# Taking the weight checks out of the first step of every chunk

## The chip, the cores and the metric

The kernel runs on one core of one Trainium2 chip. The metric is the device time of one execution in microseconds (us). Five engines work side by side, each through its own queue of instructions: TensorE for matrix products (PE in the profile, with its weight loads as PEld), VectorE (DVE), ScalarE (ACT), GpSimd (POOL), and SyncE (SP), which here issues nearly all transfers.

## The reference

An attention layer with a short window and a few always-visible first keys, followed by a two-layer network with softplus. Cut to what matters:

```python
# q, k, v: (B=4, H=8, S=768, D=64); n_sink = 4, window = 128
scores = (q @ k.transpose(0, 1, 3, 2)) / 8
keep = (key < n_sink) | ((0 <= query - key) & (query - key < window))
a = softmax(where(keep, scores, -1e9))            # over the keys
x = (a @ v).transpose(0, 2, 1, 3).reshape(3072, 512)
h = x @ w_in                                      # w_in: 512 x 2048, float64
g = maximum(h, 0) + log1p(exp(-abs(h)))
out = (g @ w_out).astype(float32)                 # w_out: 2048 x 512, float64
```

## The kernel before

The 3072 tokens are cut into 12 chunks of 256. A chunk has 8 **steps**. In step i the kernel works on two chunks at once: head i % 8 of the attention of chunk i // 8, and slice i % 8 (256 of the 2048 hidden columns) of the two dense layers of the chunk before. The loop over i is one long software pipeline; from step 17 on it runs the letters of `Ctx.STEADY` in their order. Each letter is a function and an offset. For this study these matter:

- `U` (`up`, line 474): 24 products of one slice of the first layer into the PSUM tile `h`. `F` (`softplus`, lines 481 to 483): three ScalarE passes into `mt`. `P` (`gate`, line 489, and line 50 or 48 for the cast `gh`), `R` (`residue`, `gl`, line 56): VectorE's part, of the step itself and of the step before. `D` and `E` (`down`, lines 511 to 513): 12 products of the slice of two steps before into `acc`.
- `p` (`split`): `qkh`, `kl` on line 56. `S` (`scores`): line 245 and 246. `T` (`softmax`): lines 258, 264 (VectorE) and 265 (ScalarE). `N` (`normalise`): `sm`, `rc` on VectorE (271, 272), the product with `a` on GpSimd (279).
- `W` (`weights_t`): PE turns the head's attention weights round (line 312, tile `t`), ScalarE makes the high part `th`, VectorE the low part `tl` (line 56), and GpSimd cuts both to the band with four selects (lines 323 and 326) into the tile `pt`. `V` (`values`): PE multiplies, first the sinks (line 342), then the band, which reads `pt` (line 348), both into `x`. `O` (`out`): ScalarE and VectorE (`xt` line 366, `xf` line 367) take `x` away.

Seven of eight steps run the letters in the order `kWRqpUKFSTDPNVOE`. The first step of a chunk (i % 8 = 0) runs `kqWRpSDKTUFNPVEO`: there `U` and `F` come late, behind `S`, `D` and `T`.

Behind the letters of some steps comes a **weight check** (`_weight_check`, line 455). The weights are float64 and are put together from words; one check takes the smallest and the largest magnitude of one half block of weights, two VectorE reductions of 128 x 512 into one column each of `room`. There are 32 half blocks in the list `checks`. Nobody but the flag reads `room`: `_fast_signs` in step 98 folds it with `stats` into a column, `_fast_flag` in step 100 turns that round on PE (line 697) and makes a number of it, which at the very end decides whether a slow general program has to run instead. It does not with these inputs.

PE's and SP's instructions stand in the order in which the code is written; the scheduler may arrange the rest.

Of the kernel before, what the change touches and what calls it, by code (L numbers as in the profile page):

```python
# [20 lines left out]
B, H, S, D = 4, 8, 768, 64  # L21
# [423 lines left out]
def _weight_check(c, s, k, half):  # L445

    if not c.w64:  # L450
        return
    w = c.w[s, k, half][:, 0].rearrange("p n w -> p (n w)")
    o = 2 * (2 * s + k) + half
    for e, op in enumerate((ALU.min, ALU.max)):
        c.nc.vector.tensor_reduce(c.room[:, e, o : o + 1], w, mybir.AxisListType.X, op, apply_absolute_value=True)
# [69 lines left out]
def _fast(c):  # L525
# [8 lines left out]
    lag = 2  # L534
# [11 lines left out]
    checks, dmas = list(halves), list(halves)  # L546
# [57 lines left out]
    def next_sinks(i):  # L604

        k, e = divmod(i + H, H)
        if k <= c.EXACT or k > n:
            return
        if k < n and att[k].first and 0 < e < 6:
            a = att[k]  # L610
            if e < 4:
                (a.load_sinks, a.sinks_high, a.sinks_low)[e - 1]()
            else:
                a.sinks_place(0, e - 4)
        elif att[k - 1].first and k - 1 > c.EXACT and e < 2:
            att[k - 1].sinks_place(1, e)

    def fill(n):

        for _ in range(n):  # L620
            c.nc.tensor.matmul(c.word_ps[0][:, :CT].bitcast(F32), c.sk[:, :P], c.sk[:], start=True, stop=True)
# [27 lines left out]
    with c.tc.manual_schedule():  # L649
        c.word_ps = [c.ps_acc.tile([P, WH], I32, tag=f"acc{e}", name=f"word_ps{e}") for e in range(2)]  # L650
        fill(16)
        for h in (0, 2):
            att[0].load(h)
        _constants(c)
        att[0].load_v(0)
        att[0].load_sinks()
        att[0].load(4)
        att[0].load_v(1)
        att[0].load(6)
        c.turn = 0  # L660
        c.upper = [c.lp.tile([P, WH], I32, tag=f"vs{e}", name=f"upper{e}", bufs=1) for e in range(2)]
        for t in c.upper:
            c.nc.gpsimd.memset(t[:], 0)
        for part in c.START.split():
            parts[part[0]][0](int(part[1:] or 0))
        for i in range(2 * H + 1, (n + 1) * H + lag + 1):
            for part in "JjGL" + c.STEADY[i % H == 0]:
                run, ahead = parts[part]
                run(i + ahead)
            next_sinks(i)  # L670
            if i >= 2 * H + lag and i % 2 == 0 and checks:
                _weight_check(c, *checks.pop(0))
            if i == n * H + lag:
                for e in checks:
                    _weight_check(c, *e)
                _fast_signs(c)
            if i == n * H + 2 * lag:
                _fast_flag(c)


def _fast_signs(c):

    nc = c.nc
    c.col = col = c.const.tile([P, 3], F32, name="flag_col")
    nc.vector.tensor_reduce(col[:, 0:1], c.stats[:, : c.nchunks * CH * H], mybir.AxisListType.X, ALU.max)
    for e, (op, lim, beyond) in enumerate(((ALU.min, 2.0**-119, ALU.is_lt), (ALU.max, 2.0**121, ALU.is_ge))):
        m = col[:, e + 1 : e + 2]
        nc.vector.tensor_reduce(m, c.room[:, e], mybir.AxisListType.X, op)
        nc.vector.tensor_scalar(m, m, lim, BIG, beyond, ALU.mult)
        nc.vector.tensor_tensor(col[:, 0:1], col[:, 0:1], m, ALU.max)  # L690


def _fast_flag(c):

    nc, cp = c.nc, c.const
    row = c.ps_t.tile([1, P], F32, tag="t", name="flag_row")
    nc.tensor.transpose(row[:], c.col[:, 0:1], c.ident[:])
    f = cp.tile([1, 2], F32, name="flag_f")
    ok, u = f[:, 0:1], f[:, 1:2]
    nc.vector.tensor_reduce(ok, row[:], mybir.AxisListType.X, ALU.max)  # L700
    nc.vector.tensor_scalar(ok, ok, 9.0e8, None, ALU.is_lt)
    for src, lim, op in ((c.ns, float(NS), ALU.is_le), (c.wd, 1.0, ALU.is_ge), (c.wd, float(P), ALU.is_le)):
        nc.vector.tensor_scalar(u, src[:1], lim, None, op)
        nc.vector.tensor_tensor(ok, ok, u, ALU.mult)
    c.flag = cp.tile([1, 1], I32, name="flag_i")
    nc.vector.tensor_copy(c.flag[:], ok)
# [126 lines left out]
def _kernel(tc, a, out):  # L833
# [7 lines left out]
    with ExitStack() as keep:  # L841
        c.const = keep.enter_context(tc.tile_pool(name="const", bufs=1))
        c.wp = keep.enter_context(tc.tile_pool(name="wp", bufs=1))
        c.w, c.raw, c.top, c.word = {}, {}, {}, {}
        c.ident = c.const.tile([P, P], F32, name="ident")
        c.stats = c.const.tile([P, B * H * NB], F32, name="stats")
        c.room = c.const.tile([P, 2, 4 * FP], F32, name="room")
        nc.gpsimd.memset(c.room[:], 1.0)
        c.sk = c.const.tile([P, CT], F32R, name="sk")
        ones = c.room[:].rearrange("p a b -> p (a b)").unsqueeze(1).broadcast_to([P, CT // 64, 64])  # L850
        _zero(nc, c.sk[:].rearrange("p (a b) -> p a b", b=64), ones)
        with ExitStack() as st:
            pool = lambda n, bufs: st.enter_context(tc.tile_pool(name=n, bufs=bufs))
            psum = lambda n, bufs: st.enter_context(tc.tile_pool(name=n, bufs=bufs, space=bass.MemoryType.PSUM))
            c.xp, c.mp, c.stg = pool("xp", 2), pool("mp", 2), pool("stg", 4)
            c.lp, c.ap, c.sp = pool("lp", 2), pool("ap", 2), pool("sp", 2)
            c.ps_acc, c.ps_h = psum("ps_acc", 1), psum("ps_h", 2)
            c.ps_s, c.ps_t, c.ps_x = psum("ps_s", 2), psum("ps_t", 1), psum("ps_x", 1)
            with tc.manual_schedule(engines=ORDERED):
                _fast(c)  # L860
        ok = nc.values_load(c.flag[:1, :1], min_val=0, max_val=1)
        with tc.If(ok < 1):
            _general(c)
# [77 lines left out]
```

## Time and profile before

| | |
|---|---|
| time, median of 3 runs | 724.29 us (724.26 to 725.24) |
| the profiled execution's own time | 724.42 us |
| its span, first to last instruction | 722.7 us |
| granted TensorE clock | 0.998 |
| PE / PEld / DVE / ACT / POOL busy | 97% / 86% / 80% / 63% / 52% |
| checks | 64 reductions, steps 18, 20, ... 80 |

The span is read with step numbers in mind: step 24 begins near 162 us, step 40 near 274 us, step 88 near 612 us, and a step lasts about 7 us. The last letters of `U` are those of step 103, near 705 us. Idle time that a row shows in square brackets is that of the engine just before the instruction, with what ended it.

### The profile page before, as it was taken

The numbers are of one execution on the slowest core, as the hardware profiler recorded it, in microseconds if no ns is written. First come the engines' busy times: TensorE is split into PE (matmuls) and PEld (weight loads), VectorE is DVE, ScalarE is ACT, GpSimd is POOL, SyncE is SP. The second block draws the span as 40 slices with busy tenths as digits, with TensorE's granted clock in tenths as the row PEclk, the third lists the DMA queues.
The fourth block names the chain that finished last, engine by engine and source line by source line (L and its number), as shares of the span: only waits on it lengthen the run. The fifth ranks groups of instructions, "written<-read, shape, count | busy, mean of one in ns | idle before, by whom it ended". The sixth has DMA issues, their size and how long they took to land.

```text
span 722.7 us, 13866 instructions
## 1 busy us (share of the span) xinstructions
PE 701.4 (97%) x4535; PEld 624.5 (86%) x4535; DVE 581.5 (80%) x1693; ACT 452.5 (63%) x1104; POOL 373.8 (52%) x676
## 2 busy tenths in 40 slices
PE   7889999999999999999999999999999999999996
PEld 5577789988998898998999899898888898999995
DVE  6899988888987987888888987988888887855332
ACT  4679847666666666766666666666665766643431
POOL 5867485655455564655544564564555465452000
PEclk9999999999999999999999999999999999999999
DMA  9887713221221411321321322222221312100000
GB/s 309 289 303 223 197 49 90 58 72 58 81 66 37 122 49 50 109 64 46 101 68 49 98 59 67 80 75 64 75 74 52 96 51 77 60 12 1 30 2 34
DMA packets 40875, 63.21 MB, mean 87 GB/s; under 512 B 4634, under 2 KB 22362, under 8 KB 40794
## 3 DMA queue, kind: packets, MB, share of 16 engines
q1 hardware_dynamic: 40506, 61.97, 28.0%
q8 instruction: 38, 0.62, 0.4%
q14 instruction: 43, 0.35, 0.2%
q10 hardware_dynamic: 288, 0.26, 0.1%
HBM read 55.93 MB, written 6.29 MB: 86 GB/s over the span
## 4 chain that ended last, share of the span: by engine, by line
PE 69%; DVE 14%; ACT 8%; issue 4%; POOL 3%; DMA 2%; SPq 0%; ACTq 0%; POOLq 0%; DVEq 0%
PE h L474 28%; PE acc L513 9%; PE acc L511 9%; PE acc L512 9%; PE x L348 5%; PE t L312 2%; PE s L245 2%; PE s L246 2%; DVE gl L56 2%; POOL pt L323 2%; ACT a L265 1%; PE x L342 1%; DVE kl L56 1%; ACT mt L482 1%; DVE mt L489 1%
## 5 line engine op out<-in xcount | busy, mean ns | idle before, releaser
L474 PE MATMUL h<-xh,wi 128*128 128x256 f32 x1536 | 253.8, 288 | 0.0
L474 PEld LDWEIGHTS h<-xh,wi 128*128 128x128 f32 x1536 | 211.2, 191 | 1.6 <-issue 0.5
L279 POOL TENSOR_SCALAR a<-a,rc 128x128 f32<-128x128 f32 x178 | 69.3, 402 | 188.9 <-DVE rc L272 150.5
L474 PE MATMUL h<-xl,wi 128*128 128x256 f32 x768 | 154.6, 283 | 0.0
L511 PE MATMUL acc<-wo,gh 128*128 128x512 f32 x384 | 151.8, 395 | 0.0
L513 PE MATMUL acc<-wo,gl 128*128 128x512 f32 x384 | 151.0, 393 | 0.7 <-DVE gl L56 0.7
L512 PE MATMUL acc<-wo,gh 128*128 128x512 f32 x384 | 150.7, 393 | 0.0
L474 PEld LDWEIGHTS h<-xl,wi 128*128 128x128 f32 x768 | 119.7, 192 | 0.0
L489 DVE SCALAR_TENSOR_TENSOR mt<-h,mt 128x512 f32<-128x512 f32 x96 | 66.0, 687 | 63.3 <-ACT mt L483 54.5
L481 ACT ACTIVATE mt<-h 128x512 f32<-128x512 f32 x96 | 57.1, 595 | 93.8 <-PE h L474 93.8
L265 ACT ACTIVATE a<-a,stats 128x136 f32<-128x136 f32 x192 | 76.4, 399 | 58.2 <-DVE stats L264 57.7
L513 PEld LDWEIGHTS acc<-wo,gl 128*128 128x128 f32 x384 | 72.2, 188 | 17.5 <-DVE gl L56 1.1
L511 PEld LDWEIGHTS acc<-wo,gh 128*128 128x128 f32 x384 | 72.3, 188 | 12.8 <-issue 0.3
L56 DVE TENSOR_TENSOR gl<-mt,gh 128x512 fp32r<-128x512 f32 x96 | 79.9, 832 | 0.3
L512 PEld LDWEIGHTS acc<-wo,gh 128*128 128x128 f32 x384 | 72.3, 188 | 8.9
L323 POOL TENSOR_SCALAR_AFFINE_SELECT pt<-tl 128x256 fp32r<-128x256 f32 x80 | 60.1, 751 | 29.6 <-DVE tl L56 28.9
L323 POOL TENSOR_SCALAR_AFFINE_SELECT pt<-th 128x256 fp32r<-128x256 f32 (+1 forms) x96 | 44.2, 460 | 36.1 <-ACT th L48 33.1
L482 ACT ACTIVATE mt<-mt 128x512 f32<-128x512 f32 x96 | 60.7, 633 | 3.1
L483 ACT ACTIVATE mt<-mt 128x512 f32<-128x512 f32 x96 | 60.7, 632 | 3.0
L48 ACT CAST qkh<-qk 128x656 fp32r<-128x656 f32 x80 | 59.5, 744 | 2.5 <-DMA qk<-qk 2.5
L56 DVE TENSOR_TENSOR kl<-qk,qkh 128x400 fp32r<-128x400 f32 x80 | 52.7, 658 | 2.5
L56 DVE TENSOR_TENSOR tl<-t,th 128x256 f32<-128x256 f32 x80 | 33.2, 415 | 24.5 <-ACT th L48 24.1
(185 smaller groups left out, 1245.2 us busy)
## 6 DMA issues: line engine op xcount, KB each, us to landing
qk<-qk SPq DMA_DIRECT2D x160, 164.0 KB, 3.0
vr<-v SPq DMA_DIRECT2D x32, 192.0 KB, 2.7
out<-o SPq DMA_DIRECT2D x24, 256.0 KB, 2.3
vr<-v SPq DMA_DIRECT2D x16, 128.0 KB, 2.4
q<-q SPq DMA_DIRECT2D x7, 256.0 KB, 4.6
k<-k SPq DMA_DIRECT2D x8, 200.0 KB, 4.6
wi00r<-w SPq DMA_DIRECT2D x1, 511.8 KB, 5.3
wi01r<-w SPq DMA_DIRECT2D x1, 511.8 KB
```

Of the source, the lines that this page charges most:

```text
L48: nc.scalar.copy(out, in_)
L56: (nc.vector if eng == "V" else nc.gpsimd).tensor_tensor(out, a, b, ALU.subtract)
L265: nc.scalar.activation(a, a, AF.Exp, bias=nm, scale=-1.0, accum_out=sm[:, j : j + 1])
L279: (nc.vector if eng == "V" else nc.gpsimd).tensor_scalar(a, a, rc[:, j : j + 1], 0.0, ALU.mult, ALU.add)
L323: nc.gpsimd.affine_select(pt[:, e, :, 1], src[:], [[0, CH], [1, P]], ALU.is_ge, 0.0, base=0, channel_multiplier=-1)
L474: nc.tensor.matmul(h[:, j], wt, x, start=k == 0, stop=k >= len(prods) - 2, skip_group_check=True)
L482: nc.scalar.activation(t[:], t[:], AF.Exp, scale=-1.0)
L483: nc.scalar.activation(t[:], t[:], AF.Ln, bias=1.0)
L489: nc.vector.scalar_tensor_tensor(t[:], h[:], 0.0, t[:], ALU.max, ALU.add)
L511: nc.tensor.matmul(acc[:], gh[:, j, q], wh, start=f == 0, stop=False, skip_group_check=True)
L512: nc.tensor.matmul(acc[:], gh[:, j, q], wl, start=False, stop=False, skip_group_check=True)
L513: nc.tensor.matmul(acc[:], gl[:, j, q], wh, start=False, stop=f == 2 * FP - 1, skip_group_check=True)
```

## The change

The test that starts a check is another one:

```diff
@@ -668,7 +668,7 @@
             next_sinks(i)
-            if i >= 2 * H + lag and i % 2 == 0 and checks:
+            if i >= 2 * H + lag and i % H in (2, 4, 6) and checks:
                 _weight_check(c, *checks.pop(0))
             if i == n * H + lag:
                 for e in checks:
```

Here H = 8, lag = 2 and n = 12. Before, the 32 checks sit in the even steps 18 to 80. Now the steps 24, 32, 40, 48, 56, 64, 72 and 80 have none; each check after step 22 moves to a later place, and the list lasts to step 98. Step 98 has two: the one that is its turn, and, from the loop under `i == n * H + lag`, the last one of the list. That loop takes nothing off the list, so step 100 runs the last check a second time: 33 checks, 66 reductions.

On VectorE, at the end of step 40 and the begin of step 41 (`xt`, `xf` are of step 40, `tl_1` and what follows of step 41), before:

```order
L50 CAST gh_0_3969<-mt_0_3960 128x512
L366 TENSOR_TENSOR xt_0_3985<-x_0_3971,xt_0_3985 64x256
L367 TENSOR_TENSOR xf_0_3984<-x_0_3971,xt_0_3985 64x256
L455 TENSOR_REDUCE room<-wi_732 128x1 x2
L56 TENSOR_TENSOR tl_1_3999<-t_1_3994,th_1_3997 128x256
L56 TENSOR_TENSOR gl_0_4006<-mt_0_3960,gh_0_3969 128x512
```

and now:

```order
L50 CAST gh_0_3965<-mt_0_3956 128x512
L366 TENSOR_TENSOR xt_0_3981<-x_0_3967,xt_0_3981 64x256
L367 TENSOR_TENSOR xf_0_3980<-x_0_3967,xt_0_3981 64x256
L56 TENSOR_TENSOR tl_1_3993<-t_1_3988,th_1_3991 128x256
L56 TENSOR_TENSOR gl_0_4000<-mt_0_3956,gh_0_3965 128x512
L56 TENSOR_TENSOR qkh_6_4005<-qk_6_3881,qkh_6_4005 64x256
```

The two reductions ahead of `tl_1` are gone; the rest of the row is as it was. The same is seen at the other seven first steps.

On VectorE in step 98 (`mt_2` and `gh_2` of the last chunk's third slice, then `_fast_signs`), before:

```order
L489 SCALAR_TENSOR_TENSOR mt_2_9506<-h_2_9481,mt_2_9506 128x512
L50 CAST gh_2_9519<-mt_2_9506 128x512
L685 TENSOR_REDUCE flag_col<-stats 128x1
L688 TENSOR_REDUCE flag_col<-room 128x1
L689 TENSOR_SCALAR flag_col<-flag_col 128x1
```

and now:

```order
L489 SCALAR_TENSOR_TENSOR mt_2_9502<-h_2_9477,mt_2_9502 128x512
L50 CAST gh_2_9515<-mt_2_9502 128x512
L455 TENSOR_REDUCE room<-wo_1322 128x1 x2
L455 TENSOR_REDUCE room<-wo_1347 128x1 x2
L685 TENSOR_REDUCE flag_col<-stats 128x1
L688 TENSOR_REDUCE flag_col<-room 128x1
```

Four reductions now stand ahead of the flag's work there. Two more (`wo_1347` once again) stand in step 100 ahead of line 700, and two each at the ends of the steps 82, 84, 86, 90, 92 and 94, where before there were none. PE, ACT, POOL and SP have the same instructions in the same order.

## The prediction

> **What bounds the kernel now.** I read the page first, then the waits of PE alone, then the timeline around one of them on all engines, and then the same place in a chunk that has no check.
>
> ```profile
> span 722.7 us, 13866 instructions
> PE 701.4 (97%) x4535; PEld 624.5 (86%) x4535; DVE 581.5 (80%) x1693; ACT 452.5 (63%) x1104; POOL 373.8 (52%) x676
> L455 DVE TENSOR_REDUCE room<-wi x32: 665/666/669, 126.5 to 509.0; 128x1 f32<-128x512 f32 x32
> ```
>
> PE is the bound, VectorE has a fifth of its time free, and one reduction of a check takes 0.666 us. So the change is worth something only where a check makes PE wait. The waits of PE between 115 and 640 us, which is nearly all of the steady loop, come to one row:
>
> ```profile
> engine line waited for: us in total, times, longest us
> PE x L348 <- POOL pt L326: 2.9, 8, 0.5
> ```
>
> PE waits eight times, always at `values` for the last select of `pt`. The timeline shows where: just behind the first step of a chunk. Here is the end of step 40 and step 41, VectorE first, then GpSimd, then PE:
>
> ```profile
> 282.61 0.42 DVE L367 TENSOR_TENSOR xf<-x,xt 64x256 f32<-64x256 f32 x1
> 282.95 1.26 DVE L455 TENSOR_REDUCE room<-wi 128x1 f32<-128x512 f32 x2
> 284.13 0.41 DVE L56 TENSOR_TENSOR tl<-t,th 128x256 f32<-128x256 f32 x1
> 284.61 0.80 POOL L323 TENSOR_SCALAR_AFFINE_SELECT pt<-tl 128x256 fp32r<-128x256 f32 x1 [1.74 <-DVE tl L56]
> 285.36 0.59 POOL L326 TENSOR_SCALAR_AFFINE_SELECT pt<-tl 128x256 fp32r<-128x256 f32 x1
> 285.31 0.28 PE L342 MATMUL x<-sk,vs 128*128 128x256 f32 x1
> 286.00 0.73 PE L348 MATMUL x<-pt,vv 128*128 128x256 f32 x3 [0.41 <-POOL pt L326]
> 286.57 0.40 PE L511 MATMUL acc<-wo,gh 128*128 128x512 f32 x1
> ```
>
> The check stands in VectorE's queue between `xf` of step 40 and `tl` of step 41. GpSimd sat idle 1.74 us until `tl` came, its two selects end at 285.95, and only then does PE go on. It is a chain with nothing else in it: check, `tl`, two selects, `values`.
>
> The profile holds its own counter-example. The last check before runs in step 80, so the chunk boundary at step 88 is the same program without a check:
>
> ```profile
> 620.83 0.42 DVE L367 TENSOR_TENSOR xf<-x,xt 64x256 f32<-64x256 f32 x1
> 621.17 0.40 DVE L56 TENSOR_TENSOR tl<-t,th 128x256 f32<-128x256 f32 x1
> 621.64 0.80 POOL L323 TENSOR_SCALAR_AFFINE_SELECT pt<-tl 128x256 fp32r<-128x256 f32 x1 [0.55 <-DVE tl L56]
> 622.40 0.59 POOL L326 TENSOR_SCALAR_AFFINE_SELECT pt<-tl 128x256 fp32r<-128x256 f32 x1
> 623.53 0.28 PE L342 MATMUL x<-sk,vs 128*128 128x256 f32 x1
> 623.64 0.63 PE L348 MATMUL x<-pt,vv 128*128 128x256 f32 x3
> 624.11 0.39 PE L511 MATMUL acc<-wo,gh 128*128 128x512 f32 x1
> ```
>
> Reckoned from `xf`, `tl` starts 0.34 us later here and 1.52 us later there: the check costs the chain 1.18 us. Without it the selects end at 622.99, and PE wanted them at 623.64: 0.65 us in hand, no wait.
>
> **What is removed: eight checks in first steps.** From the start of line 342 to that of line 511, PE takes 286.57 - 285.31 = 1.26 us with the check and 624.11 - 623.53 = 0.58 us without: 0.68 us lost, of which the row calls 0.41 idle. The other 0.27 us is hidden in how rows are drawn (line 342 is drawn 0.28 long though its successor could start after 0.11) and in the first product behind a wait, which runs without its usual overlap. So each wait costs its idle time plus 0.27. Over the eight: 2.9 + 8 x 0.27 = 5.1 us. All eight have a check of a first step ahead of them (steps 24 to 80, the places that the change empties), and the last, smaller one has the same shape:
>
> ```profile
> 567.01 0.28 PE L342 MATMUL x<-sk,vs 128*128 128x256 f32 x1
> 567.58 0.73 PE L348 MATMUL x<-pt,vv 128*128 128x256 f32 x3 [0.29 <-POOL pt L326]
> ```
>
> Three chunks, those whose attention begins a new batch (steps 24, 48, 72), have a second, smaller delay one step on, too short for the list of waits. In step 26, and for comparison in step 27:
>
> ```profile
> 179.79 0.47 POOL L326 TENSOR_SCALAR_AFFINE_SELECT pt<-tl 128x128 fp32r<-128x128 f32 x1
> ...
> 180.07 0.28 PE L342 MATMUL x<-sk,vs 128*128 128x256 f32 x1
> ...
> 180.77 0.39 PE L511 MATMUL acc<-wo,gh 128*128 128x512 f32 x1
> ...
> 187.11 0.28 PE L342 MATMUL x<-sk,vs 128*128 128x256 f32 x1
> ...
> 187.57 0.39 PE L511 MATMUL acc<-wo,gh 128*128 128x512 f32 x1
> ```
>
> 0.70 against 0.46 us: 0.24 each, 0.7 in all. The selects were 0.07 us late: they end at 180.26, and PE can go on 0.12 after the start of line 342 (623.64 - 623.53), at 180.19. I count this as gone too. The reason is the slack one step after the boundary with and without the check, in step 42 and in step 90:
>
> ```profile
> 292.24 0.59 POOL L326 TENSOR_SCALAR_AFFINE_SELECT pt<-tl 128x256 fp32r<-128x256 f32 x1
> 292.93 0.28 PE L342 MATMUL x<-sk,vs 128*128 128x256 f32 x1
> ...
> 629.28 0.59 POOL L326 TENSOR_SCALAR_AFFINE_SELECT pt<-tl 128x256 fp32r<-128x256 f32 x1
> 630.46 0.28 PE L342 MATMUL x<-sk,vs 128*128 128x256 f32 x1
> ```
>
> The selects are done 0.10 us before line 342 starts with the check (292.83), 0.59 before without (629.87). Half a microsecond more covers 0.07. Its two bounds are 0 and 0.7 us; I take 0.7.
>
> Sum of what goes: 5.1 + 0.7 = 5.8 us.
>
> **What is added: checks in later steps.** Steps 82, 84 and 86 are the twins of steps 34, 36 and 38, which have checks now and no PE wait (the eight waits of the row are all taken by boundaries). Steps 90, 92 and 94 are like 42, 44 and 46, or lighter, since the next chunk's loads and scores have run out. In step 43, right behind the check of step 42, the selects end at 299.12 and PE asks for them 0.74 us later at the earliest:
>
> ```profile
> 298.53 0.59 POOL L326 TENSOR_SCALAR_AFFINE_SELECT pt<-tl 128x256 fp32r<-128x256 f32 x1
> 299.86 0.28 PE L342 MATMUL x<-sk,vs 128*128 128x256 f32 x1
> ```
>
> That cover is not used up by a PE that comes earlier: PE comes 0.68 us earlier at step 41, VectorE's chain 1.18 us. So these cost 0. If the cover were gone, each could cost what a boundary costs, 0.68.
>
> Steps 98 and 100 carry six reductions, 6 x 0.666 = 4.0 us of VectorE, in a part where VectorE has this:
>
> ```profile
> 682.72 0.35 DVE L685 TENSOR_REDUCE flag_col<-stats 128x1 f32<-128x192 f32 x1
> 683.94 0.68 DVE L56 TENSOR_TENSOR gl<-mt,gh 128x512 fp32r<-128x512 f32 x1
> 687.27 0.69 DVE L489 SCALAR_TENSOR_TENSOR mt<-h,mt 128x512 f32<-128x512 f32 x1 [2.65 <-ACT mt L483]
> 691.20 0.39 PE L513 MATMUL acc<-wo,gl 128*128 128x512 f32 x1
> 693.48 0.27 PE L697 MATMUL flag_row<-ident,flag_col 128*1 128x128 f32 x1
> 695.48 0.67 DVE L56 TENSOR_TENSOR gl<-mt,gh 128x512 fp32r<-128x512 f32 x1
> 698.62 0.69 DVE L489 SCALAR_TENSOR_TENSOR mt<-h,mt 128x512 f32<-128x512 f32 x1 [2.47 <-ACT mt L483]
> ```
>
> In step 98 four reductions (two take 1.18 us of queue, so 2.4) stand ahead of `gl`, which then ends near 687.0. The next `mt` starts at 687.27 anyway, and PE reads that `gl` at 691.20. The flag's column is then ready near 686.3, seven us before line 697. In step 100, 1.2 us goes into the 2.47 us of idle time behind `gl`. Cost 0; the whole of it, were nothing hidden, would be 4.0 us. The 33rd check is dead work in that same gap. No transfer and no other engine's instruction moves, so no queue besides VectorE's is touched.
>
> **The sum.** 724.42 (the profiled execution's own time) - 5.8 = 718.6 us. That execution lay 0.13 above the median of the runs shown, so against the median it is 718.5 us, 0.8% less. About 0.2%, 1.45 us, is what can be told from no change here.
>
> A row that speaks against all this is the page's 97% for PE: taken as a bound, at most 3% is to be had anywhere, and VectorE at 80% is not the engine to relieve. The Trainium skill, "Perfetto Trace Analysis", section "Identifying the Most-Contended Engine", would have one optimise the engine of the highest occupancy first, and judge TensorE by its weight loads rather than by its matmul rows. By that the 86% of PEld still stands above VectorE's 80%, and relieving VectorE would give 0: 724.3. By the row of waits it gives 5.8, and the sum goes by the row.
>
> **The rivals.**
>
> 1. *Only part of the wait goes.* Behind `tl` something else is late at the boundary, such as GpSimd's own selects of `th`, so that `pt` comes at the same time or half as much earlier. Against it: step 89 shows no such thing. Half of 5.8 gives 721.4.
> 2. *Nothing changes, since PE is full:* what PE gains at a boundary it gives back at the next wait of the chunk. This is the reading by occupancy. For it speaks the 97%; against it, that the steps after 41 have no wait of PE in which to give it back. 724.3.
> 3. *The tail is not hidden.* `gl` of step 98 comes late for line 513 and all 4.0 us show at the end. It decides once the delay passes 691.20 - 684.62 = 6.6 us; it is 2.4. 718.5 + 4.0 = 722.5.
> 4. *Slower: the wait moves to the other check steps.* The pause at the boundary is what lets VectorE catch up; without it the lag lasts, and the steps behind the checks of steps 2 and 4 of a chunk wait instead. In nine chunks (steps 26 to 92) 18 waits of 0.68 are 12.2 us, less 5.8: 730.7. The point from which it decides is a lag above the 0.74 us of step 43. Against it: VectorE gains 1.18 at the boundary where PE gains 0.68, so the lag shrinks.
>
> **How the numbers follow.** The forecast, all eight waits and the three small ones gone and nothing put in their place, has 0.86; rival 1 has 0.06, rival 2 has 0.04, rival 3 has 0.02, rival 4 has 0.02. The forecast's own spread: 0.7 up if the small delays stay, and another 1 us up because one of the three runs before lay that far above the others (725.24); 0.6 down if a small stall of the boundaries that I did not count goes as well. That makes 717.8 to 720.4, and holds nine tenths of 0.86. Taking in a little of rival 1, up to 720.8, brings it to 8 in 10. Faster by over 0.2%: 0.86 + 0.06 + 0.02 = 0.94; within 0.2%: 0.04; slower: 0.02.
>
> **What the profile afterwards would show.** The list of PE's waits between 115 and 640 us is empty, or has nothing at line 348. At step 40, `tl` follows `xf` at once, GpSimd's idle time ahead of its select of `tl` falls from 1.74 to some 0.55 us, and from line 342 to line 511 PE takes 0.58 us. The tail from 660 us on keeps its length, with six reductions in VectorE's idle time. VectorE's busy time rises by 1.3 us. It would be wrong if PE's wait at line 348 stayed with another releaser, if waits turned up at steps 3 or 5 of a chunk, or if line 513 waited for `gl` in the tail.

## The result, and the profile after

| | before | after |
|---|---|---|
| time, median (lowest to highest) | 724.39 us (724.26 to 725.24, 4 runs) | 718.01 us (717.56 to 718.19, 4 runs) |
| ratio | | 0.9911, 95% interval 0.9898 to 0.9923 |
| profiled execution, its span | 724.42, 722.7 us | 717.56, 715.8 us |
| DVE busy | 581.5 us x1693 | 581.5 us x1695 |

The kernel is 6.4 us faster, 0.9%. The page after, its first lines and that of the chain that ended last:

```profile
span 715.8 us, 13868 instructions
PE 697.6 (97%) x4535; PEld 624.0 (87%) x4535; DVE 581.5 (81%) x1695; ACT 451.9 (63%) x1104; POOL 373.5 (52%) x676
PE 91%; DVE 4%; ACT 2%; POOL 1%; DMA 1%; issue 1%; ACTq 0%; POOLq 0%
```

PE's share of that chain was 69% before and is 91% now; VectorE's fell from 14% to 4%. The list of PE's waits between 115 and 640 us, which had one row with 2.9 us, has no row any more. The boundary of step 40 and 41 after the change (VectorE, GpSimd, PE):

```profile
280.11 0.42 DVE L367 TENSOR_TENSOR xf<-x,xt 64x256 f32<-64x256 f32 x1
280.46 0.41 DVE L56 TENSOR_TENSOR tl<-t,th 128x256 f32<-128x256 f32 x1
280.93 0.80 POOL L323 TENSOR_SCALAR_AFFINE_SELECT pt<-tl 128x256 fp32r<-128x256 f32 x1 [0.55 <-DVE tl L56]
281.69 0.59 POOL L326 TENSOR_SCALAR_AFFINE_SELECT pt<-tl 128x256 fp32r<-128x256 f32 x1
282.82 0.28 PE L342 MATMUL x<-sk,vs 128*128 128x256 f32 x1
282.93 0.63 PE L348 MATMUL x<-pt,vv 128*128 128x256 f32 x3
283.40 0.39 PE L511 MATMUL acc<-wo,gh 128*128 128x512 f32 x1
```

This is row for row the counter-example of the prediction, step 88: GpSimd idle 0.55 us instead of 1.74, the selects done 0.65 us before PE needs them, 0.58 us from line 342 to line 511.

Where the time went shows best in the starts of the products of `up`, which mark every step. From step 16 to step 96 the two profiles run 561.31 us before and 555.10 us after: 6.21 us less. The boundary steps (from the first slice of `up` to the third) are shorter by 0.51, 0.79, 0.68, 0.52, 0.79, 0.68, 0.52 and 0.58 us, the second delays of the steps 26, 50 and 74 by 0.23, 0.22 and 0.24. That is 5.76 us. Another 0.35 is a single pause near 556 us (below), and 0.1 lies in differences of a few hundredths. The start up to step 16 was 0.91 us shorter in this execution and the tail 0.26 longer, all of it behind PE's last product. PE's rows in that stretch are busy 558.30 us before and 555.10 after, and its idle time falls from 3.01 us to nothing. The instructions are the same, so about half of what a wait costs is drawn as busy time.

### The profile page after: what moved, and what is told of

Same layout as the page of the kernel before. It is cut to its first block, busy times and chain, and to the rows that moved or that the text cites. A ratio compares the mean times of both kernels' runs of the same rounds, so it can differ in the third digit from the quotient of the medians.

```text
span 715.8 us, 13868 instructions
## 1 busy us (share of the span) xinstructions
PE 697.6 (97%) x4535; PEld 624.0 (87%) x4535; DVE 581.5 (81%) x1695; ACT 451.9 (63%) x1104; POOL 373.5 (52%) x676
## 4 chain that ended last, share of the span: by engine, by line
PE 91%; DVE 4%; ACT 2%; POOL 1%; DMA 1%; issue 1%; ACTq 0%; POOLq 0%
PE h L474 37%; PE acc L513 12%; PE acc L511 12%; PE acc L512 12%; PE x L348 6%; PE s L245 3%; PE t L312 3%; PE s L246 3%; PE x L342 2%; DVE wt L418 1%; PE ts L296 1%; DMA words<-sizes 1%; PE s L242 1%; POOL wi L56 0%; ACT upper L48 0%
## 5 line engine op out<-in xcount | busy, mean ns | idle before, releaser
L56 DVE TENSOR_TENSOR gl<-mt,gh 128x512 fp32r<-128x512 f32 x96 | 78.9, 822 | 0.3
```

The costliest lines, as they stand in the source:

```text
L56: (nc.vector if eng == "V" else nc.gpsimd).tensor_tensor(out, a, b, ALU.subtract)
```

## The experiments

All were made from one of the two kernels, and each is timed against runs of the kernel before on its own chip. The two theories of the first call: **A**, a check costs time only where it stands ahead of `tl` in a step with too little slack; **B**, what counts is how many reductions VectorE has per chunk.

**e1, no checks at all** (trigger and the loop in step 98 taken out).

> Leaves out all 32 checks of the weights (64 reductions of VectorE); the flag's work stays. Theory A (a check costs time only where it stands ahead of tl in a step whose slack is too small): as the changed kernel, 718.0 us (717.5 to 718.5), no wait of PE at line 348, since the 24 other checks and the six reductions of the tail cost 0. Theory B (VectorE's load per chunk is what counts): taking away four checks per chunk instead of one brings several times the 6.4 us that one brought, below 710 us.

719.58 us against 723.86, ratio 0.9944 (0.9928 to 0.9961). Theory B is dead, and A's "the others cost 0" as well: without any check the kernel is *slower* than the changed one with its 33 (the intervals of the two ratios lie apart). From step 16 to 96 it takes 557.00 us, 1.90 more than the changed kernel, nearly all of it in the steps 20, 22, 44, 46, 68 and 70 (0.14 to 0.46 each), and PE has three waits again:

```profile
PE x L348 <- POOL pt L326: 0.5, 3, 0.2
```

VectorE and GpSimd in step 21 of this kernel:

```profile
140.51 0.43 DVE L56 TENSOR_TENSOR tl<-t,th 128x256 f32<-128x256 f32 x1
140.54 0.61 POOL L174 TENSOR_TENSOR vs<-vsh,hmask 64x256 fp32r<-64x256 f32 x1
140.85 3.27 DVE L56 TENSOR_TENSOR gl<-mt,gh 128x512 fp32r<-128x512 f32 x1
141.11 0.40 POOL L323 TENSOR_SCALAR_AFFINE_SELECT pt<-th 128x256 fp32r<-128x256 f32 x1
141.47 0.40 POOL L326 TENSOR_SCALAR_AFFINE_SELECT pt<-th 128x256 fp32r<-128x256 f32 x1
141.83 0.40 POOL L323 TENSOR_SCALAR_AFFINE_SELECT pt<-tl 128x256 fp32r<-128x256 f32 x1
142.19 0.40 POOL L326 TENSOR_SCALAR_AFFINE_SELECT pt<-tl 128x256 fp32r<-128x256 f32 x1
142.56 1.01 POOL L56 TENSOR_TENSOR vv<-vr,vv 128x384 fp32r<-128x384 f32 x1
```

and PE in step 22:

```profile
151.90 0.38 PE L348 MATMUL x<-pt,vv 128*128 128x256 f32 x1 [0.17 <-POOL pt L326]
```

`gl` takes 3.27 us where 0.67 is usual, here and near 308 and 476 us. It reads two tiles and runs beside six GpSimd instructions that stand back to back; it ends 0.55 us after the last of them. What is behind it on VectorE is late, and one step on, in step 22, PE waits at line 348. That the one brings the other is put to the test in e8.

**e8, three checks put back** (`if i in (20, 44, 68) and checks`, nothing else).

> The kernel without checks, but the three of the steps 20, 44 and 68 put back; leaves out the 29 other checks. Theory C (in those steps a check holds tl and gl back while GpSimd does its selects; without it gl, which reads two tiles, starts beside them and takes 3.27 us, and what is late behind it makes PE wait two steps on): the 3.3 us rows of gl near 141, 308 and 476 us are gone, the waits at line 348 too, and the time falls by the 1.9 us that the steady part lost: 719.6 - 1.9 = 717.7 us. Six more reductions make the kernel faster. Rival: the program without checks is slower for another reason (where its instructions lie, or the spread of the start): it stays at 719.6 us.

718.02 us, ratio 0.9917 (0.99 to 0.9933): six more reductions make the kernel 1.6 us faster. The two intervals overlap a little, so the profile has to decide: from step 16 to 96 it takes 555.53 us, 1.47 less than without, PE's waits at line 348 are gone, and the 0.4 that the steps 22, 46 and 70 lost each is back. 0.08 to 0.20 stays in the steps 20, 44 and 68. A `gl` of 2.8 to 2.9 us stands in the step ahead of each (near 127, 293 and 460 us), in e1 and in e8; whether it is the cause was not tested. VectorE at the end of step 20 and in step 21, and GpSimd's first select of `tl`:

```profile
140.27 1.26 DVE L455 TENSOR_REDUCE room<-wi 128x1 f32<-128x512 f32 x2
141.45 0.41 DVE L56 TENSOR_TENSOR tl<-t,th 128x256 f32<-128x256 f32 x1
141.79 0.67 DVE L56 TENSOR_TENSOR gl<-mt,gh 128x512 fp32r<-128x512 f32 x1
141.93 0.80 POOL L323 TENSOR_SCALAR_AFFINE_SELECT pt<-tl 128x256 fp32r<-128x256 f32 x1
```

The check acts as a spacer: it holds `tl` back, GpSimd has to wait for `tl` between its selects, and `gl` starts in that gap. Now GpSimd pays, with 0.80 us for a select that took 0.40 in e1. The kernels before and after both have this check, so the change did not touch it. The Trainium skill, "SBUF — State Buffer", section "Who interferes with whom", says that a VectorE instruction with two SBUF inputs contends with a GpSimd instruction that reads SBUF, that the port pair they share is an exclusive lock, and that `tensor_reduce` never contends on this chip. The rows agree: `gl` takes 3.27 or 0.67 us, and of the 64 reductions of the kernel before, the 48 that ran beside GpSimd took 0.667 us in the mean, the 16 others the same. (In e5 all 64 ran beside GpSimd, at 0.675 to 0.687.)

**e2, the check of the first step ahead of the gate.**

```diff
+                if part == "P" and i > 2 * H + lag and i % H == 0 and checks:
+                    _weight_check(c, *checks.pop(0))
                 run, ahead = parts[part]
...
-            if i >= 2 * H + lag and i % 2 == 0 and checks:
+            if i >= 2 * H + lag and i % H in (2, 4, 6) and checks:
```

> All 32 checks in the same steps as in the kernel before; only in the first step of a chunk the check stands ahead of the gate, where VectorE sat idle 1.44 us waiting for ScalarE, not behind xf. Theory A: the 1.18 us fit into that idle time, tl comes as early as without a check: 718.0 us (717.5 to 718.8), no wait of PE at line 348. Theory B: four checks per chunk as before, 724.3 us.

717.47 us, ratio 0.9913 (0.9896 to 0.9929), the same gain with all 32 checks in the same steps as before. Not the step and not the amount matters but the place in VectorE's queue:

```profile
277.11 0.17 DVE L272 RECIPROCAL rc<-sm 128x2 f32<-128x2 f32 x1
277.19 1.26 DVE L455 TENSOR_REDUCE room<-wi 128x1 f32<-128x512 f32 x2
278.72 0.69 DVE L489 SCALAR_TENSOR_TENSOR mt<-h,mt 128x512 f32<-128x512 f32 x1 [0.27 <-ACT mt L483]
280.23 0.42 DVE L367 TENSOR_TENSOR xf<-x,xt 64x256 f32<-64x256 f32 x1
280.57 0.41 DVE L56 TENSOR_TENSOR tl<-t,th 128x256 f32<-128x256 f32 x1
```

The two reductions went into the time that VectorE waited for ScalarE's `mt`; 0.27 of it is left, and `tl` follows `xf` after 0.34 us.

**e3, half a check** (in the kernel before, of the first step's check one reduction stays and the other goes to the end of the second step).

> The kernel before, but of the check of a chunk's first step only one reduction stays there, and the other goes to the end of the second step. Theory A: tl is delayed by 0.59 us where 0.65 was in hand (0.54 in some chunks), so almost nothing waits: 718.0 to 719.5 us, likeliest 718.5. If each reduction costs its share of the wait (proportional): half of the gain, 721.2 us. Theory B: 724.3 us.

718.98 us, ratio 0.9935 (0.9918 to 0.9951), within A's range and 2.2 below the proportional reading. No wait of PE is long enough to be listed. `tl` starts 0.59 us later than without a check. Against the changed kernel the boundaries of the chunks that begin a batch lost nothing, where the changed kernel has 0.83 us in hand. The steps 40 and 64 lost 0.10 and 0.12, where it has 0.66, the steps 32 and 56 lost 0.23 and 0.21, where it has 0.52, and the steps 26, 50 and 74 lost 0.15 to 0.16. (Another 0.35 is the pause told of at the end; it lies ahead of the boundary of step 80, where nothing was lost.) So the loss follows what exceeds the slack and not a share of the check, but it begins some 0.15 us before the slack is used up.

**e4, a double check in the first step** (`i % H in (0, 4, 6)`, two of them where `i % H == 0`).

> From step 24 on the checks of a chunk's first and third step both stand at the end of the first step (step 80 has one, as before); the number of checks per chunk is as before. Theory A: the chain check, tl, selects, values is already late, so all of the second check shows: seven boundaries by 1.18 us, 724.4 + 8.3 = 732.7 us (731.5 to 734). Theory B: 724.4 us, since the load is the same.

733.51 us, ratio 1.0135 (1.0118 to 1.0151). Its waits of PE:

```profile
PE x L348 <- POOL pt L326: 11.3, 8, 1.7
PE x L342 <- DVE sk L56: 0.5, 2, 0.3
```

The seven boundaries with two checks are each 1.18 to 1.21 us longer than with one, 8.4 in all, as expected to a tenth. The rest is a new wait that nobody had expected, line 342 for `sk` in the steps 44 and 68, 0.63 us each; what makes `sk` late there was not looked for.

**e5, all checks in the odd steps** (`i % 2 == 1`), and **e9, the same without the last step of a chunk** (`i % H in (1, 3, 5)`).

> The kernel before with its 32 checks in the odd steps 19 to 81, so four per chunk, none in a chunk's first step, one in its second. Theory A: the check of the second step stands ahead of a tl that VectorE waits 0.70 us for anyhow, so it delays it by some 0.48, where 0.7 us is in hand without a check; the slack behind the checks of the other odd steps is larger. 718.0 us, up to 719.2 if the chunks that begin a batch have less in hand. Theory B (load per chunk): 724.4 us.

728.39 us, ratio 1.0055 (1.0039 to 1.0072): a miss by 10 us, and the change's opposite, though it also clears the first step. PE's waits:

```profile
PE ts L296 <- DVE tl L56: 7.4, 8, 1.0
PE x L348 <- POOL pt L326: 0.4, 2, 0.2
PE x L342 <- DVE sk L56: 0.3, 1, 0.3
```

I had looked at the slack of `values` alone. `tl` also empties `t`, the one PSUM tile for turned matrices, and in a chunk's first step PE next wants that tile for the sinks (line 296). A check at the end of the last step stands ahead of that `tl`.

> The checks in the steps 19, 21, then the second, fourth and sixth step of a chunk: the kernel with odd steps without the check of the last step. Theory D (the check of a chunk's last step holds back tl of the next, which frees the one PSUM tile t that the sinks' transposes need): PE's eight waits at line 296 (7.4 us, 8.7 us with what rows hide) are gone. What stays is the 2 us of theory C, since steps 20, 44 and 68 have no check: 728.4 - 8.7 = 719.7 us, 718.9 to 720.5. Rival: checks in odd steps cost wherever they stand, so a quarter less of the loss against the changed kernel: 718.0 + 0.75 x 10.4 = 725.8 us.

720.02 us, ratio 0.9943 (0.9927 to 0.996), as expected to 0.3: the waits at line 296 are gone, and what is left are three short waits at line 348, those of the missing spacers in the steps 20, 44 and 68.

**e6, three boundary checks put back** into the changed kernel (`i % H in (2, 4, 6) or i in (24, 48, 72)`).

> The changed kernel with a check put back into the steps 24, 48 and 72 alone (the first steps of the chunks whose attention begins a batch); the list then ends in step 92. Theory A, with the small second delays counted to the check as predicted: 3 x (0.51 + 0.24) = 2.2 us on top of 718.0, 720.2 us, PE's waits at line 348 three, at the places 173, 341 and 510 us. If the second delays do not come from the check: 719.5 and the changed kernel shows them too. Theory B: less than 0.5 us.

720.54 us, ratio 0.9945 (0.9929 to 0.9962). The three boundary steps lost 0.51, 0.52 and 0.51 us, and the steps 26, 50 and 74 lost 0.22, 0.24 and 0.66. So the second delay does come from the check. The third is larger, and the trace shows by what. In the steps 26 and 50 `gl` takes 1.21 us and GpSimd's select of `th` beside it 0.40. In step 74 it is the other way round, and the selects end too late for PE:

```profile
513.30 0.68 DVE L56 TENSOR_TENSOR gl<-mt,gh 128x512 fp32r<-128x512 f32 x1
513.32 0.92 POOL L323 TENSOR_SCALAR_AFFINE_SELECT pt<-th 128x256 fp32r<-128x256 f32 x1
515.67 0.62 PE L348 MATMUL x<-pt,vv 128*128 128x512 f32 x2 [0.38 <-POOL pt L326]
```

In step 50, too, `gl` starts 0.02 us ahead of that select, so the starts that the profile shows do not tell which of the two will be held.

**e7, eight checks in step 98** (`and i <= 80 and checks`).

> The changed kernel, but the list is left at step 80, and its last 8 checks (16 reductions, 9.4 us) all stand in step 98. Prediction's rival 3 with its point: gl of step 98 ends 9.4 us later than it did (684.62 to 694.06 in the clock of the kernel before), and line 513 wants it at 691.20: PE waits 2.9 us, 718.0 + 2.9 = 720.9 us; up to 5 us (723.0) if the next mt, which is late too, holds back the next step. If the tail hides whatever stands in it: 718.0 us.

722.08 us, ratio 0.9968 (0.9955 to 0.998), with a wide spread (720.32 to 723.2, 8 runs). The row is the expected one:

```profile
687.58 0.50 PE L513 MATMUL acc<-wo,gl 128*128 128x512 f32 x1 [2.81 <-DVE gl L56]
```

2.81 us against 2.9, 3.07 with what rows hide. So the tail does not hide whatever stands in it: it has room for the delay worked out in the prediction and no more. The median is another 1 us higher than that accounts for. In the profiled execution, 719.9 us of span, no other wait of PE shows: against that of the changed kernel 3.07 us are this wait, 0.55 lie before step 16 and 0.44 behind PE's last product. The two executions at a granted clock of 0.999 took 720.32 and 720.48 us, the six at 0.992 to 0.998 took 721.67 to 723.2, so the spread goes in part with the clock; what lowered it was not looked for.

## Why the prediction was right, point by point

- *The place and the chain.* Right. With the check gone from between `xf` and `tl`, all eight waits went, and e2 shows that the place in the queue alone does it.
- *5.1 us for the eight waits, 0.27 on top of each row.* Right: the eight boundary steps are 5.07 us shorter.
- *0.7 us for the three second delays.* Right: 0.69, and e6 brings them back with the check.
- *Added checks at 0.* Right for the steps 82 to 94 and for the tail. In step 98 `gl` came at 679.19 for a product at 684.08, and the next `mt` still waited 0.28 us for ScalarE, close to the 0.2 that the sum left:

```profile
675.60 2.46 DVE L455 TENSOR_REDUCE room<-wo 128x1 f32<-128x512 f32 x4
679.19 0.69 DVE L56 TENSOR_TENSOR gl<-mt,gh 128x512 fp32r<-128x512 f32 x1
680.15 0.69 DVE L489 SCALAR_TENSOR_TENSOR mt<-h,mt 128x512 f32<-128x512 f32 x1 [0.28 <-ACT mt L483]
684.08 0.39 PE L513 MATMUL acc<-wo,gl 128*128 128x512 f32 x1
```

- *VectorE's busy time up by 1.3 us.* Wrong: it stayed at 581.5. The two more reductions are there, but `gl` fell from 79.9 to 78.9 us in all: behind the checks that now stand in the steps 84, 86, 90, 92 and 94 it takes 0.67 to 0.68 us, where without a check it took 0.93 to 0.94.
- *718.5 us.* It was 718.0, inside the range. Most of the difference is the pause of 0.35 us at 556 us, which the sum did not hold and for which the range's lower end alone left room ("a small stall of the boundaries that I did not count"). That it is gone as well is luck. What is left is 0.1 us in small differences and the spread of the executions: the start up to step 16 alone was 0.4 to 0.9 us shorter in every kernel profiled after the first, and with one profile of the kernel before it is not shown that any of this belongs to the change. The terms given for the range add up to 717.9 and 720.2 us rather than 717.8 and 720.4.
- *The rivals.* The first two predicted waits that stay, and there are none. That PE is full at 97% was no bound: PE's own busy time fell from 701.4 to 697.6 us with the same instructions, 3.20 us of it from step 16 to 96, since part of a wait is drawn as busy. The third has its deciding point where it was put (e7). The fourth did not come.
- *What was right by luck.* "A check in a later step costs 0" was read off the waits of `values`. e5 shows a step, the last of a chunk, where the same reading fails for another tile, and e1 and e8 show three steps where a check is worth 1.5 us together.

## What to carry to other kernels

Price a piece of movable work by its place in its engine's queue: by what stands behind it, and by the slack of *everyone* who waits for that, the next user of a PSUM tile included. The best place is ahead of an instruction that waits anyway; there the whole 1.2 us of a check was free (e2). A stretch of the same program without the piece, here the boundary at step 88, gives the price before anything is run.

## What the runs showed that was not expected

Work that is taken away can cost time. In e1 VectorE's two-input subtraction `gl` starts three times beside a run of GpSimd instructions and is held until that run is over, 3.27 us instead of 0.67. A check ahead of it avoids that: three checks more, 1.5 us less from step 16 to 96 (e1, e8). It is not always held so long. In the kernel before, `gl` of step 22 (148.72 us) takes 2.12 us and gets in ahead of the last of five GpSimd instructions, and that select then takes 0.85 us instead of 0.40.

VectorE makes a pause of 0.26 us that no semaphore explains, once in some of the kernels:

```profile
556.47 0.43 DVE L56 TENSOR_TENSOR tl<-t,th 128x256 f32<-128x256 f32 x1 [0.26 <-issue]
```

In the kernel before, e2, e3 and e4 it stands ahead of the same instruction, number 1423 of VectorE's records, and in e6 ahead of number 851, also a `tl` in a chunk's first step; PE loses 0.35 us there (0.21 in e6) at line 296. In the changed kernel and the others no such pause shows. It goes with the place in the instruction stream and not with the time, 550 to 566 us. In all five traces a packet of 8 KB on the queue q14, which the page of the profile lists as one of instructions, starts 0.66 to 0.70 us after the pause ends. Over thirty such packets run in each traced kernel, most without a pause, so the fetching of instructions is a candidate for the cause and no more; it was not tested.
